# Storing the weight combinations of gate, up and Q in the first token half and loading them in the second

## Chip, cores, metric

One core of one Trainium2 chip. The metric is the device time of one execution in microseconds (us). The time before is 733.7 us, the median of three runs (732.07 to 734.33); with the runs made beside the changed kernel it is 732.96.

## The reference

```python
def reference(A_x, A_wqkv, A_wo, B_x, B_w_gate, B_w_up, B_w_down):   # S = 2048, D = 1024, F = 3584
    x = A_x
    xn = _layernorm(x)
    s = linear_attention(xn, A_wqkv, A_wo)      # 32 heads, phi(q), phi(k), kv and z sums over tokens; cut
    g = silu((silu(xn @ B_w_gate) * (xn @ B_w_up)) @ B_w_down)
    return x + s * g                            # bf16
```

## The kernel before

The kernel does its matrix products by a seven-product (Strassen-like) scheme. Each product of a 2x2 block matrix needs *combinations* of weight blocks (sums and differences), made by VectorE (DVE), and combinations of the results, read from PSUM. For the products "1" and "5" of gate, up and Q the scheme is applied a second time (the code calls it `joint`), so these need *inner* combinations too.

The tokens are worked off in two halves `p = 0, 1`. Order of the work: K and V and their state (0 to about 134 us), then for each half Q/gate/up in pairs of column tiles and after it the down-projection. Every weight tile of gate, up and Q is loaded twice, and its combinations are made twice. This is the part that the change touches:

```python
def sums(A, o, rd, wr):                      # four DVE subtractions or additions
    tt(rd, [wr[0]], o[0], A[0, 1], A[1, 1], ALU.add, True)
    tt(rd + [wr[0]], [wr[1]], o[1], o[0], A[0, 0], ALU.subtract, True)
    tt(rd, [wr[2]], o[2], A[0, 0], A[0, 1], ALU.subtract, True)
    tt(rd + [wr[1]], [wr[3]], o[3], A[1, 0], o[1], ALU.subtract, True)

def wload(src, joint):
    s = raw_ring.take()                      # 8 KB a partition, the raw tile, 1 MB
    dma([], [s.r], ..., src, dsem("wr%d" % s.k), 1024 * KB)
    c = cmb_ring.take()                      # 8 KB a partition: the outer combinations
    sums({...}, [cv[:, q] for q in range(4)], [s.r], cr)          # 4 x 128x1024
    # ... cut
    for m in joint:                          # (1, 5), or () for the very first Q tile
        t = in_ring.take()                   # 2 KB a partition: inner combinations
        sums(A, [tv[:, q] for q in range(4)], [r], tr)            # 4 x 128x256
```

The kernel does not issue its instructions in the order of this code. It collects all of them and runs a *list scheduler* in the build: a small model of five engines and one DMA queue decides the order of the instructions on each engine. Each engine then works strictly through that order on the chip, waiting on semaphores. The model has a rate for DMA, and a lead time for loads. (The byte count of a transfer enters a second time, in the deadline by which it is to be issued: 4.0 us + bytes / 200e3 before its first use. That line was not changed.)

```python
for o in ops:                                # every DMA: not before this PE instruction
    if o.sem is not None and o.succs:
        k = bisect_right(cum, o.dl - self.lead) - 1
        if k >= 0 and pes[k] not in o.preds:
            o.preds.add(pes[k])
# ... cut; in the loop that places one instruction after the other:
            if o.sem is not None:
                free[e] = s + 0.08
                b = max(s + 1.0, dma_free)
                dma_free = b + o.nbytes / 230e3      # MODELLED bytes per us of the one queue
                o.done = dma_free + 1.8
```

In the third pair of tiles (`n == 2`) of each half, the kernel also normalises Q: it reads reciprocals back from DRAM with a partition broadcast (`H<-r_scratch`, 16 transfers of 128 KB a half) and writes Q to `q_scratch` (2 MB a half).

## Time and profile before

| | before |
|---|---|
| time, median | 733.7 us |
| PE (TensorE) busy | 717.3 of 731.5 us, 98% |
| DVE busy | 596.5 us, 82% |
| ACT (ScalarE) busy | 397.7 us, 54% |
| DMA traffic | 94.0 MB |

The page of the kernel before: busy times and, in 40 slices, the tenths of PE and DVE and the granted clock.

```profile
span 731.5 us, 10526 instructions
...
PE 717.3 (98%) x3894; PEld 365.9 (50%) x3894; DVE 596.5 (82%) x1395; ACT 397.7 (54%) x743; POOL 14.1 (2%) x35
...
PE   8999999999999999999999999999999999999996
...
DVE  6999868979989998787457889999899988757353
...
PEclk9999999999999999999999999999999999999999
```

PE is busy everywhere, DVE nearly so in the Q/gate/up stages. The windows view of two stretches of the second half's Q/gate/up (columns: busy time and number of instructions of PE, PEld, DVE, ACT and POOL, then the granted clock, the DMA share, GB/s):

```profile
440.00:460.00 20.00, 19.46 (x113) 10.73 (x112) 20.00 (x52) 13.14 (x27) 0.00 (x0) 1.00 0.44 134
540.00:600.00 60.00, 60.00 (x349) 33.97 (x348) 55.76 (x139) 36.61 (x76) 0.00 (x0) 1.00 0.42 136
```

In the first, DVE is busy for all 20 us and PE loses 0.5. In the second, DVE is busy for 93% and PE loses nothing.

### The profile page before, as it was taken

The page shows a single profiled execution, that of the slowest core. Times are in us where ns is not written, and L with a number is a line of the kernel's source. Part 1 is how long each engine was busy: PE and PEld are TensorE (multiplying, and loading weights), DVE is VectorE, ACT ScalarE, POOL GpSimd, SP SyncE. Part 2 cuts the span into 40 slices and gives each one's busy share as a digit, 9 for nine tenths or more (in the row PEclk, how much of TensorE's full clock was granted, in tenths as well). Part 3 has the DMA queues.
Part 4 walks back from the last instruction along what each step waited for, and adds up shares of the span by engine and source line. Part 5 has one row for each costly group of instructions (what it writes and reads, how often), then busy time and mean ns, then how long its engine had stood idle before and what let it go on. Part 6 is the DMA issues. An engine that isn't in the chain of part 4 may idle for free.

```text
span 731.5 us, 10526 instructions
## 1 busy us (share of the span) xinstructions
PE 717.3 (98%) x3894; PEld 365.9 (50%) x3894; DVE 596.5 (82%) x1395; ACT 397.7 (54%) x743; POOL 14.1 (2%) x35
## 2 busy tenths in 40 slices
PE   8999999999999999999999999999999999999996
PEld 3444445455555555544444455555455554444442
DVE  6999868979989998787457889999899988757353
ACT  3776654787659766623232376767786654223231
POOL 2111000000000000000000000000000000000000
PEclk9999999999999999999999999999999999999999
DMA  9443235135257432471846534132835245274822
GB/s 293 110 102 86 44 111 176 59 109 166 75 149 217 156 109 65 130 216 32 213 118 153 170 86 152 59 116 76 245 145 173 74 136 167 77 166 118 177 65 50
DMA packets 135219, 94.00 MB, mean 129 GB/s; under 512 B 32512, under 2 KB 131072, under 8 KB 135168
## 3 DMA queue, kind: packets, MB, share of 16 engines
q1 hardware_dynamic: 135168, 93.34, 44.9%
q8 instruction: 30, 0.49, 0.3%
q14 instruction: 21, 0.17, 0.1%
HBM read 75.50 MB, written 10.62 MB: 118 GB/s over the span
## 4 chain that ended last, share of the span: by engine, by line
PE 86%; DVE 6%; ACT 4%; DMA 2%; issue 1%; POOL 0%; SPq 0%; ACTq 0%; DVEq 0%
PE ps L210 86%; ACT TM L341 2%; ACT H L341 2%; DMA W<-in_B_w_up_dram 1%; DVE H L717 1%; DVE W L348 1%; DVE ps L348 1%; DVE stats L642 1%; DVE TM L348 1%; DVE H L348 1%; ACT L341 1%; DVE TM L716 0%; DVE stats L646 0%; DMA W<-in_A_x_dram 0%; ACT ps L341 0%
## 5 line engine op out<-in xcount | busy, mean ns | idle before, releaser
L210 PE MATMUL ps<-X,W 128*128 128x512 f16 (+1 forms) x1408 | 312.0, 361 | 0.9 <-DVE ps L348 0.5
L341 ACT ACTIVATE TM<-ps 128x512 f16<-128x512 f32 (+2 forms) x337 | 181.7, 556 | 152.6 <-PE ps L210 148.5
L210 PE MATMUL ps<-H,W 128*128 128x512 f16 (+1 forms) x896 | 206.8, 379 | 0.3 <-DVE ps L348 0.3
L210 PEld LDWEIGHTS ps<-X,W 128*128 128x128 f16 (+1 forms) x1408 | 136.6, 98 | 122.2 <-DVE ps L348 2.3
L348 DVE TENSOR_TENSOR W<-W 128x256 f16<-128x256 f16 (+6 forms) x424 | 169.1, 440 | 9.7 <-DMA W<-in_B_w_down_dram 5.7
L348 DVE TENSOR_TENSOR ps<-ps,TM 128x256 f32<-128x256 f32 (+1 forms) x218 | 117.1, 540 | 33.1 <-PE ps L210 32.2
L210 PEld LDWEIGHTS ps<-H,W 128*128 128x128 f16 (+1 forms) x896 | 87.2, 98 | 103.4 <-DVE ps L348 0.7
L341 ACT ACTIVATE ps<-ps 128x512 f32<-128x512 f32 (+1 forms) x156 | 78.6, 504 | 59.3 <-PE ps L210 55.6
L341 ACT ACTIVATE H<-ps 128x512 f16<-128x512 f32 (+1 forms) x126 | 74.9, 602 | 57.4 <-PE ps L210 57.2
L210 PE MATMUL ps<-P,W 128*128 128x256 f16 (+1 forms) x440 | 90.0, 323 | 0.1
L210 PE MATMUL ps<-W 128*128 128x256 f16 (+1 forms) x328 | 69.7, 299 | 2.2 <-DVE ps L348 1.7
L348 DVE TENSOR_TENSOR TM<-ps,TM 128x512 f32<-128x512 f32 (+1 forms) x60 | 40.8, 681 | 29.4 <-PE ps L210 28.8
L341 ACT ACTIVATE TM<-TM 128x512 f16<-128x512 f32 (+1 forms) x61 | 37.9, 621 | 44.1 <-DVE TM L348 43.6
L210 PEld LDWEIGHTS ps<-P,W 128*128 128x128 f16 (+1 forms) x440 | 42.9, 98 | 32.9 <-DVE H L717 0.5
L348 DVE TENSOR_TENSOR H<-H,TM 128x512 f16<-128x512 f16 x112 | 45.2, 417 | 12.7 <-ACT H L341 12.4
L348 DVE TENSOR_TENSOR H<-H 128x1024 f16<-128x1024 f16 (+2 forms) x82 | 50.5, 629 | 0.6 <-DMA H<-in_A_wqkv_dram 0.3
L210 PEld LDWEIGHTS ps<-W 128*128 128x128 f16 (+1 forms) x328 | 30.8, 98 | 27.9 <-DVE ps L348 3.5
L348 DVE TENSOR_TENSOR TM<-TM 128x512 f16<-128x512 f16 (+1 forms) x59 | 24.2, 419 | 18.3 <-DMA TM<-TM 10.7
L210 PE MATMUL ps<-H,X 128*128 128x512 bf16 (+1 forms) x136 | 32.2, 379 | 1.2 <-ACT X L341 0.8
L210 PE MATMUL ps<-TM,W 128*128 128x256 f16 (+1 forms) x144 | 30.9, 296 | 0.3 <-DVE ps L348 0.3
L348 DVE TENSOR_TENSOR W<-H 128x1024 f16<-128x1024 f16 x40 | 26.9, 685 | 3.0 <-PE ps L210 2.8
L716 DVE TENSOR_SCALAR TM<-TM 128x512 f16<-128x512 f16 x64 | 17.7, 285 | 10.3 <-ACT TM L341 10.1
(81 smaller groups left out, 413.1 us busy)
## 6 DMA issues: line engine op xcount, KB each, us to landing
W<-in_B_w_gate_dram SPq DMA_DIRECT2D x14, 1024.0 KB, 5.3
W<-in_B_w_up_dram SPq DMA_DIRECT2D x14, 1024.0 KB, 5.5
W<-in_B_w_down_dram SPq DMA_DIRECT2D x16, 896.0 KB, 6.1
W<-in_A_x_dram SPq DMA_DIRECT2D x16, 256.0 KB, 3.0
H<-in_A_wqkv_dram SPq DMA_DIRECT2D x8, 512.0 KB, 8.3
W<-in_A_wqkv_dram SPq DMA_DIRECT2D x4, 1024.0 KB, 5.2
H<-r_scratch SPq DMA_DIRECT2D x32, 128.0 KB, 4.0
q_scratch<-H SPq DMA_DIRECT2D x8, 512.0 KB, 4.0
```

The source lines that it names most:

```text
L210: last = h.matmul(o, l, r, start=st, stop=sp, skip_group_check=True)
L341: return PL.op("act", reads, writes, lambda h: h.activation(o, i, func, **kw), nel(o) / 1200.0 + (0.055 if src == "ps" else 0.095))
L348: return dve(reads, writes, lambda h: h.tensor_tensor(o, a, b, op), nel(o), 1.92 if fast else 0.96)
L642: o0 = dve([s.r], [sA], lambda h: h.bn_stats(stats[:, j, 0, :], xa[:, 0:512]), 512)
L716: dve([e.r], [b.r], lambda h: h.tensor_scalar(ba, ea, 1.0, EPS_PHI, ALU.min, ALU.add), 512, 2.6)
L717: dve([src_r, b.r], [out_r], lambda h: h.scalar_tensor_tensor(out_ap, src, 0.0, ba, ALU.max, ALU.add), 512)
```

## The change

Intent: make the combinations once, in the first half, store them in DRAM (1 MB a tile, and two times 256 KB of inner ones), and load them in the second half, so that DVE has less to do there. The two constants of the scheduler's model were raised with it. The swap of two PSUM allocations in `Joint.step` came along too. Core of the diff:

```diff
-                dma_free = b + o.nbytes / 230e3
+                dma_free = b + o.nbytes / 320e3
-def build_kernel(nc, ..., LEAD=12.0):
+def build_kernel(nc, ..., LEAD=16.0):
+        c_scr = nc.dram_tensor("c_scratch", [16, 128, 4096], FP16)
+        i_scr = nc.dram_tensor("i_scratch", [16, 2, 128, 1024], FP16)
@@ Joint.step @@
-                    self.x, self.y = balloc(), balloc(True)
-                    x, y = self.x, self.y
+                    y = self.y = balloc(True)
+                    x = self.x = balloc()
@@
+        kept = {}
+        def combine(p, key, t, scr, make):
+            if key in kept:
+                dma([named(*key)], [t.r], t.ap(FP16), scr, dsem("cl..."), t.size * 128)      # load
+                return
+            make()
+            if p == 0:
+                kept[key] = True
+                dma([t.r], [named(*key)], scr, t.ap(FP16), dsem("cs..."), t.size * 128)      # store
@@ wload @@
-            sums({...}, [cv[:, q] for q in range(4)], [s.r], cr)
+            combine(p, ("c", n), c, c_scr[n], lambda: sums({...}, ...))
-                sums(A, [tv[:, q] for q in range(4)], [r], tr)
+                combine(p, ("i", n, m), t, i_scr[n, ...], partial(sums, A, ...))
```

The diff also brings code for a third joint product, "6" (`put6`, `LINK6`, places for its inputs). The lists that would switch it on stay `((1, 5), (1, 5))`, so it never runs.

More of the change, by code (lines that the diff above doesn't have):

```diff
@@ L218, in _tr_group, with build_kernel @@
     return last
-def build_kernel(nc, A_x, A_wqkv, A_wo, B_w_gate, B_w_up, B_w_down, out, WINDOW=6, NWARM=14, NPE=4, LEAD=12.0):
+def build_kernel(nc, A_x, A_wqkv, A_wo, B_w_gate, B_w_up, B_w_down, out, WINDOW=6, NWARM=14, NPE=4, LEAD=16.0):
     S, D, FF = 2048, 1024, 3584
@@ L480, in grp @@
                     pe_mm(reads, [bank_r[b]], mms)
+            s1_ring = None
             def put1(self, a):
                 self.a = a
+                if self.s1_ring is not None:
+                    self.s1 = self.s1_ring.take()
+                    act([bank_r[a]], [self.s1.r], self.s1.ap(F32), ps[a][:, :], ACT.Identity)
+                    return
                 self.b = balloc()
@@ L490, in put5, with put6, add5 @@
                 bfree(e)
+            def put6(self, b):
+                self.b = b
+                tt([bank_r[b], self.s1.r], [bank_r[b]], ps[b][:, :], ps[b][:, :], self.s1.ap(F32), ALU.add)
+                self.add5()
+            def add5(self):
+                self.c = balloc()
+                tt([bank_r[self.b], self.s5.r], [bank_r[self.c]], ps[self.c][:, :], ps[self.b][:, :],
+                   self.s5.ap(F32), ALU.add)
             def step(self, m):
@@ L505, in step @@
                     self.grp(6, self.b, False)
-                    self.c = balloc()
-                    tt([bank_r[self.b], self.s5.r], [bank_r[self.c]], ps[self.c][:, :], ps[self.b][:, :],
-                       self.s5.ap(F32), ALU.add)
+                    self.add5()
                 elif m == 7:
@@ L524, in build_kernel @@
         QJ = (((), (1, 5)), ((1, 5), (1, 5)))
+        GJ = ((1, 5), (1, 5))
         class Joint:
@@ L582, in build_kernel @@
         LINK = "7_0 nj1a 3_0 7_1 nj1b nj5a 3_1 nj1c nj5b 4_0 nj1d nj5c 4_1 n2_0 nj5d n6_0 n2_1 n6_1".split()
+        LINK6 = ("nj1a 7_0 3_0 nj1b nj5a 7_1 nj1c 3_1 nj5b nj1d nj6a 4_0 nj5c nj6b 4_1 nj5d nj6c n2_0 nj6d n2_1").split()
         last_pair = [None]
@@ L595, in feed @@
             else:
-                for w in LINK:
+                for w in LINK6 if "6" in pair.joint else LINK:
                     if w[0] == "n":
@@ L933, in build_kernel, with wload @@
         SUM_OF = {5: 0, 6: 1, 7: 2, 3: 3}
-        def wload(src, joint):
+        kept = {}
+        def combine(p, key, t, scr, make):
+            if key in kept:
+                dma([named(*key)], [t.r], t.ap(FP16), scr, dsem("cl%s%d" % (t.a.name, t.off // KB)), t.size * 128)
+                return
+            make()
+            if p == 0:
+                kept[key] = True
+                dma([t.r], [named(*key)], scr, t.ap(FP16), dsem("cs%s%d" % (t.a.name, t.off // KB)), t.size * 128)
+        def wload(p, n, src, joint):
             s = raw_ring.take()
@@ L943, in wload @@
             cr = [c.sub(q * 2 * KB, 2 * KB).r for q in range(4)]
-            sums({(k, i): v[:, :, 4 * k:4 * k + 4, i * 128:i * 128 + 128] for k in range(2) for i in range(2)},
-                 [cv[:, q] for q in range(4)], [s.r], cr)
+            combine(p, ("c", n), c, c_scr[n], lambda: sums(
+                {(k, i): v[:, :, 4 * k:4 * k + 4, i * 128:i * 128 + 128] for k in range(2) for i in range(2)},
+                [cv[:, q] for q in range(4)], [s.r], cr))
             def block(m):
@@ L962, in wload @@
                 A = {(k, i): bl[:, i, 2 * k:2 * k + 2, :] for k in range(2) for i in range(2)}
-                sums(A, [tv[:, q] for q in range(4)], [r], tr)
+                combine(p, ("i", n, m), t, i_scr[n, (1, 5).index(m)] if m < 6 else None,
+                        partial(sums, A, [tv[:, q] for q in range(4)], [r], tr))
                 inner[m] = (A, r, tv, tr)
@@ L978, in xset, with x_inner, joint_of @@
             return Set(ops, evac, dring)
-        IN_AT = (((W, 48 * KB), (W, 49 * KB), (W, 50 * KB)), ((W, 51 * KB), (TM, 8 * KB), (TM, 9 * KB)))
+        IN_AT = {1: (None, (W, 48 * KB), (W, 49 * KB), (W, 50 * KB)), 5: (None, (W, 51 * KB), (TM, 8 * KB), (TM, 9 * KB)),
+                 6: ((X, 10 * KB), (X, 11 * KB), (X, 12 * KB), (X, 13 * KB))}
+        s1_places = Places([(X, 14 * KB), (TM, 24 * KB)], 2 * KB)
         xin = {}
-        def x_inner(v):
-            for m, at in zip((1, 5), IN_AT):
+        def x_inner(v, ms):
+            for m in ms:
                 ap, r = v[XOF[m]]
                 B = {(k, j): ap[:, 2 * k:2 * k + 2, 256 * j:256 * j + 256] for k in range(2) for j in range(2)}
-                t = [(a.at(o, KB, FP16).rearrange("p (k t) -> p k t", t=256), a.reg(o, KB)) for a, o in at]
-                tt([r], [t[1][1]], t[1][0], B[1, 1], B[0, 1], ALU.subtract, True)
-                tt([r], [r], B[0, 1], B[0, 1], B[0, 0], ALU.subtract, True)
-                tt([r], [t[0][1]], t[0][0], B[1, 1], B[0, 1], ALU.subtract, True)
-                tt([r, t[0][1]], [t[2][1]], t[2][0], B[1, 0], t[0][0], ALU.subtract, True)
-                xin[m] = {1: (B[0, 0], r), 2: (B[1, 0], r), 3: (B[1, 1], r), 5: (B[0, 1], r), 6: t[0], 7: t[1], 4: t[2]}
-        def joint_of(jstat, s0, s1):
+                t1, t2, t3, t4 = ((B[0, 1], r) if at is None else
+                                  (at[0].at(at[1], KB, FP16).rearrange("p (k t) -> p k t", t=256), at[0].reg(at[1], KB))
+                                  for at in IN_AT[m])
+                tt([r], [t3[1]], t3[0], B[1, 1], B[0, 1], ALU.subtract, True)
+                tt([r], [t1[1]], t1[0], B[0, 1], B[0, 0], ALU.subtract, True)
+                tt([r, t1[1]], [t2[1]], t2[0], B[1, 1], t1[0], ALU.subtract, True)
+                tt([r, t2[1]], [t4[1]], t4[0], B[1, 0], t2[0], ALU.subtract, True)
+                xin[m] = {1: (B[0, 0], r), 2: (B[1, 0], r), 3: (B[1, 1], r), 5: t1, 6: t2, 7: t3, 4: t4}
+        def joint_of(jstat, s0, s1, ms):
             def ops(m):
@@ L1001, in ops @@
                 return f
-            return {"1": Joint(ops(1), lambda w, b: (s0, s1)[w].put1(b)),
-                    "5": Joint(ops(5), lambda w, b: (s0, s1)[w].put5(b))}
+            if 6 in ms:
+                s0.s1_ring = s1.s1_ring = s1_places
+            return {str(m): Joint(ops(m), lambda w, b, m=m: getattr((s0, s1)[w], "put%d" % m)(b)) for m in ms}
         later = deque()
@@ L1021, in q_load @@
         def q_load(p, s):
-            return wload(wqkv_v[:, :, s * 512:(s + 1) * 512], QJ[p][s])
+            return wload(p, 14 + s, wqkv_v[:, :, s * 512:(s + 1) * 512], QJ[p][s])
         PQ0 = 52 * KB
@@ L1039, in q_pair @@
             s0, s1 = (xset(stat, w, XV[p], evac(w), d_ring) for w in range(2))
-            pair = Pair(s0, s1, joint_of(jstat, s0, s1) if QJ[p][s] else None, at)
+            pair = Pair(s0, s1, joint_of(jstat, s0, s1, QJ[p][s]) if QJ[p][s] else None, at)
             if go:
@@ L1107, in hb2, with gu_load @@
             return v, Region(hb(n, nm)[1].keys + hb(n + 1, nm)[1].keys)
-        def gu_load(k, n):
-            return wload((wg_v if k == "g" else wu_v)[:, :, n * 512:(n + 1) * 512], (1, 5))
+        def gu_load(p, k, n):
+            return wload(p, 7 * (k == "u") + n, (wg_v if k == "g" else wu_v)[:, :, n * 512:(n + 1) * 512], GJ[p])
         sgs = {}
@@ L1143, in gu_pair @@
                 s0.direct, s1.direct = direct(0), direct(1)
-            feed(Pair(s0, s1, joint_of(jstat, s0, s1), at))
+            feed(Pair(s0, s1, joint_of(jstat, s0, s1, GJ[p]), at))
         def h_sums(n):
@@ L1328, in pump @@
                 k, p, s = lq.popleft()
-                got[k, p, s] = q_load(p, s) if k == "q" else gu_load(k, s)
+                got[k, p, s] = q_load(p, s) if k == "q" else gu_load(p, k, s)
         pump(2)
@@ L1343, in turn_pass @@
             combos(XV[1])
-            x_inner(XV[1])
+            x_inner(XV[1], (1, 5))
             gate[0] = 1
@@ L1372, in build_kernel @@
                 if (p, k, n) == (0, "q", 0):
-                    x_inner(XV[0])
+                    x_inner(XV[0], (1, 5))
                 pump(1)
```

## The prediction

> **What bounds the kernel now.** TensorE's instruction stream. The page's busy table gives PE 717 of 731.5 us (98%), DVE 596 (82%), ACT 398 (54%); the clock row is 9 throughout. A busy PE need not be at its peak, so I looked at matmul starts in the timeline: back to back, a 512-column matmul starts every 216 ns, a 256-column one every 108. The Trainium skill ("TensorE: Matmul & The Clock Gate", Part 1) states N/2.4 GHz plus about 2.5 ns for a warm array, 215.7 ns at 512; this trace agrees. Summing start-to-start time above those spacings gives PE's real slack: about 5 us in the first 32 us, 2.6 near 133-139 us (start of the first half's Q/gate/up), about zero in both down-projection stages (306-420, 610-722), 5.0 in the second half's Q/gate/up (422-610), 2.3 at the end. In 422-610 the pieces are 1.5 us at 521 and 0.1-0.7 each at 422, 432, 435, 443, 469, 479, 531-534.
>
> **What the change does.** The joint products stay (1, 5) for every pair and the joint-6 code is never reached, so every matmul stays. In the second half it removes the DVE sums of 16 weight tiles: four 128x1024 at 681 ns and, for gate/up and one Q tile, eight 128x256 at 281 ns: 4.97 us of a pair's 11.7, about 77 us in all. DVE should fall from 596 to about 520 us, and its share in 540-600 us from 93% to 50-55%. It adds about 23.5 MB of stores in the first half and as much of loads in the second: DMA traffic from 94 to about 143 MB. It also starts loads up to 4 us earlier (LEAD) and swaps two PSUM allocations.
>
> **How much is on the critical path.** Almost none. The 77 us can buy at most the 5 us above (0.7%). I expect 2 to 3: the waits at 431-443 and 469-479, where DVE is full (the windows view shows 20.0 of 20 us in 440-460), should go. The wait at 521 differs: a 1 MB up-weight load took 9.9 us to land instead of 5.5, because the broadcasts from r_scratch were in the queues, and DVE, then PE, waited.
>
> **What it may cost.** A second-half pair now needs 2.5 MB in place of 1 MB per 11.7 us, 224 GB/s. The DMA share and GB/s columns put full queues at about 300-330 GB/s for weight loads (my estimate from 0.82 at 251 and 0.32 at 105), so the steady state fits at about 70%. At n=2 the broadcasts (2 MB, about 200 GB/s while all engines are busy) and q_scratch stores (2 MB) come on top: an estimated 33 us of DMA work in two pairs, 23 us. The inner-combination buffers free only about one pair before use. I expect stalls of 1 to 4 us around 510-535 us in place of today's 1.5, and up to 2 us in the first half, where stores share one queue with loads and SP waits in order for DVE.
>
> **Prediction.** Gains and stalls nearly cancel: 732.5 us, 8 in 10 between 727.5 and 739. Faster by over 2%: 0.01; within 2%: 0.94; slower by over 2%: 0.05.
>
> **What would show it.** Right: matmul count equal, PE busy within 1% of 717, DVE near 520, DMA near 143 MB, the small PE waits before 480 us gone, the down-projection stages equally long. The balance is decided around 510-535 us: PE waiting there for scratch or weight loads. Wrong if PE waits for loads in the steady state (540-600 us), the queue order or true DMA rate being worse than I think (slower); or if matmul spacing falls when DVE is lighter (faster), of which the down-projection stages, DVE light and spacing 216 ns too, show nothing.

## The result

| | before | after |
|---|---|---|
| median of 4 runs | 732.96 us | 737.61 us |
| ratio | | 1.0063, 95% interval 1.0043 to 1.0083 |
| span of the profiled run | 731.5 | 736.5 |
| DVE busy | 596.5 | 543.7 |
| DMA traffic | 94.0 MB | 143.3 MB |

A ratio is the mean time of one kernel's fast runs over that of the other's of the same rounds, so it is not quite the ratio of the medians. The changed kernel is 4.65 us slower. The page after:

```profile
span 736.5 us, 10437 instructions
...
PE 716.4 (97%) x3880; PEld 366.6 (50%) x3894; DVE 543.7 (74%) x1211; ACT 396.6 (54%) x743; POOL 14.3 (2%) x35
...
PE   7999999899999999999999989999999999999996
...
DVE  6999867979989998796447775856875568746443
...
PEclk9999999999999999999999999999999999999999
```

The number of weight loads (PEld) is 3894 in both, so TensorE's work is the same. (14 matmul records are missing from the second trace.) 184 DVE instructions went, as expected. The same two windows after:

```profile
440.00:460.00 20.00, 20.00 (x118) 11.39 (x117) 11.46 (x25) 14.65 (x30) 0.00 (x0) 1.00 0.79 265
540.00:600.00 60.00, 60.00 (x350) 34.06 (x349) 37.26 (x75) 38.39 (x81) 0.00 (x0) 1.00 0.77 270
```

DVE fell from 93% to 62% in the steady state, the DMA share rose from 0.42 to 0.77, and PE lost nothing in either case. So neither the gain nor the loss is there.

**Where the time went.** Both traces hold all 3894 weight loads in their order, and the total work up to the end of a stage is the same. So the start of the k-th weight load in one trace less that in the other is the lag at that point. (Within a stage the order differs, and lags of a few tenths mean nothing.) I worked these lags out of the timeline:

| point (k-th weight load) | before, at us | after lags by |
|---|---|---|
| end of the K/V stage (720) | 133.9 | 0.2 us |
| first half, before the broadcasts (1200) | 215.8 | 0.2 |
| first half, after them (1440) | 256.9 | 2.3 |
| second block of its down-projection (2040) | 373.8 | 2.3 |
| near its end (2280) | 423.8 | 3.9 |
| second half, after the turn (2400) | 446.8 | 4.8 |
| second half, before its broadcasts (2760) | 505.0 | 4.3 |
| after them (3000) | 547.7 | 2.8 |
| second down-projection (3480) | 636.0 | 2.8 |
| last weight load (3893) | 727.1 | 4.0 |

After the last weight load 1.0 us more is lost in the order of the last outputs (4.4 us to the end before, 5.4 after). In the second half 1.9 us came back between 2400 and 3000 (before rounding). (That this is the freed DVE would be too quick: e1 below, with all sums still made, regains 1.9 us there, most of it because the up-weight load is no longer late.) They were more than eaten by losses in places where the change has no combinations to load: the first half's broadcasts (2.1), the two down-projections (1.6 and 1.2), and the end (1.0). At the turn into the second half another 0.9 went.

The loss of 1.6 us in the first down-projection shows its mechanism. First, before, around 385 us: DMA issues on SP, then DVE. (A line of the timeline has the start, the duration, the engine, the line of the code, the operation, output<-input, and in brackets how long the engine stood idle before it and who ended that.)

```profile
378.35 0.37 SPq L351 DMA_DIRECT2D W<-in_B_w_down_dram  x1
378.77 2.43 SPq L1250 DMA_TRANSPOSE TM<-TM  x1
381.24 0.58 SPq L351 DMA_DIRECT2D W<-m_scratch  x1
381.86 0.89 SPq L351 DMA_DIRECT2D W<-in_B_w_down_dram  x1
```

```profile
385.26 0.70 DVE L348 TENSOR_TENSOR ps<-ps,TM 128x512 f32<-128x512 f32 x1 [5.56 <-PE ps L210]
385.87 0.41 DVE L348 TENSOR_TENSOR TM<-TM 128x512 bf16<-128x512 f16 x1
387.40 0.43 DVE L348 TENSOR_TENSOR TM<-TM 128x512 f16<-128x512 f16 x1 [1.12 <-ACT TM L341]
387.75 1.55 DVE L348 TENSOR_TENSOR W<-W 128x512 f16<-128x512 f16 x4
391.31 0.69 DVE L348 TENSOR_TENSOR TM<-ps,TM 128x512 f32<-128x512 f32 x1 [2.01 <-PE ps L210]
391.92 1.69 DVE L348 TENSOR_TENSOR W<-W 128x896 f16<-128x896 bf16 x3
```

DVE first serves PSUM (`ps<-ps`), makes the combinations of the small matrix (`128x512`), and comes to those of w_down (`128x896`) last, at 391.9, without waiting for either load. After:

```profile
378.55 1.56 SPq L353 DMA_DIRECT2D W<-in_B_w_down_dram  x2
380.90 4.55 SPq L1289 DMA_TRANSPOSE TM<-TM  x1
385.49 0.60 SPq L353 DMA_DIRECT2D W<-m_scratch  x1
```

```profile
388.23 0.62 DVE L350 TENSOR_TENSOR W<-W 128x896 f16<-128x896 bf16 x1 [6.90 <-DMA W<-in_B_w_down_dram]
388.78 0.42 DVE L350 TENSOR_TENSOR TM<-TM 128x512 bf16<-128x512 f16 x1
389.11 0.62 DVE L350 TENSOR_TENSOR W<-W 128x896 f16<-128x896 bf16 x1
389.65 0.69 DVE L350 TENSOR_TENSOR ps<-ps,TM 128x512 f32<-128x512 f32 x1
...
390.40 0.82 PE L210 MATMUL ps<-H,W 128*128 128x512 f16 x3 [1.39 <-DVE ps L350]
```

The scheduler has put the w_down combinations ahead of the PSUM addition. DVE waits 6.9 us in order for a load that landed late, the PSUM addition stands behind it, and PE waits 1.39 us for that addition. The second w_down load landed at 388.2, 9.0 us after its issue. In the kernel before it landed later still, at 389.9 (8.0 us after its issue), and delayed nobody, because DVE came to it only at 391.9. Over the whole trace, DVE's waits for w_down went from 5.7 us in 3 places to 21.9 in 5.

The other clear change of order is at the first half's broadcasts. SP before, then after:

```profile
211.39 0.40 SPq L351 DMA_DIRECT2D W<-in_B_w_up_dram  x1
214.20 5.62 SPq L351 DMA_DIRECT2D H<-r_scratch  x8
```

```profile
210.50 1.74 SPq L353 DMA_DIRECT2D H<-r_scratch  x4
212.29 0.43 SPq L353 DMA_DIRECT2D W<-in_B_w_up_dram  x1
214.39 2.17 SPq L353 DMA_DIRECT2D H<-r_scratch  x4
```

Four broadcasts now go ahead of the up-weight load. In after, DVE waited 1.6 us for that load between 205 and 240 us, and PE 1.5 us for DVE; before, neither waited there.

### The profile page after: what moved, and what is told of

The parts are those of the page before. It is cut to its first block, busy times and chain, and to the rows that moved or that the text cites. A ratio compares the mean times of both kernels' runs of the same rounds, so it can differ in the third digit from the quotient of the medians.

```text
span 736.5 us, 10437 instructions
## 1 busy us (share of the span) xinstructions
PE 716.4 (97%) x3880; PEld 366.6 (50%) x3894; DVE 543.7 (74%) x1211; ACT 396.6 (54%) x743; POOL 14.3 (2%) x35
## 4 chain that ended last, share of the span: by engine, by line
PE 82%; DMA 7%; DVE 4%; ACT 4%; issue 1%; SPq 1%; ACTq 0%; DVEq 0%
PE ps L210 82%; DMA W<-in_B_w_down_dram 3%; ACT H L343 1%; ACT TM L343 1%; DMA W<-i_scratch 1%; DMA H<-in_A_wqkv_dram 1%; DVE ps L350 1%; DMA W<-m_scratch 1%; DMA H<-r_scratch 1%; DVE W L350 1%; SPq L353 1%; DVE H L350 1%; DVE H L736 1%; DMA W<-in_A_x_dram 1%; DVE TM L350 1%
## 5 line engine op out<-in xcount | busy, mean ns | idle before, releaser
L350 DVE TENSOR_TENSOR W<-W 128x256 f16<-128x256 f16 (+6 forms) x284 | 121.4, 463 | 28.1 <-DMA W<-in_B_w_down_dram 21.9
L210 PEld LDWEIGHTS ps<-P,W 128*128 128x128 bf16 (+1 forms) x440 | 42.8, 98 | 34.8 <-DVE TM L350 2.0
L350 DVE TENSOR_TENSOR H<-ps,TM 128x512 f16<-128x512 f32 (+1 forms) x35 | 24.0, 685 | 3.3 <-PE ps L210 2.3
```

The costliest lines, as they stand in the source:

```text
L210: last = h.matmul(o, l, r, start=st, stop=sp, skip_group_check=True)
L350: return dve(reads, writes, lambda h: h.tensor_tensor(o, a, b, op), nel(o), 1.92 if fast else 0.96)
```

## Experiments

Twelve kernels were run; all but e4 and e12 gave correct results. "Before" in each measurement is the kernel before, run in the same rounds. My first theory (A) was: the stores cost the first half its 2 us, the scheduler's constants cost the down-projections their 3. Rivals: all of the loss is DMA traffic (B), or all of it is the constants (C). The code of the constants can be changed without the scratch and the other way round, so the two were crossed.

### e1: only the constants

```diff
 (kernel before)
-                dma_free = b + o.nbytes / 230e3
+                dma_free = b + o.nbytes / 320e3
-LEAD=12.0
+LEAD=16.0
```

> The kernel before with only the scheduler's two constants of the change (LEAD 16, DMA model 320). Theory A (traffic and constants share the loss: stores cost 2 us at 222-236 us of the first half, constants about 2.8 us in the down-projection stages at 388, 660 and 700 us and 1 at the end): 2 to 4 us slower than before, with the same stalls of PE waiting for w_down combinations in the down-projection stages. Rival B (all the loss is DMA traffic): 733, no change, no stall in the down-projection stages. Rival C (constants alone explain everything): 737 to 738.

Measured: 737.28 us, ratio 1.0063 (1.0050 to 1.0076). That is the whole loss of the change, without a byte of scratch. B falls, and A was too small on this side. The profile (of a run at 735.9, the fastest of the six) has the stall in the down-projection that after has. DVE's waits in 366 to 400 us of e1:

```profile
DVE W L348 <- DMA W<-in_B_w_down_dram: 7.2, 1, 7.2
```

It also loses 3.0 us at the first half's broadcasts (k = 1200 to 1440), so the stores of the scratch are not what after lost there.

### e2: the scratch with the constants of before

```diff
 (kernel after)
-                dma_free = b + o.nbytes / 320e3
+                dma_free = b + o.nbytes / 230e3
-LEAD=16.0
+LEAD=12.0
```

> The kernel after with the scheduler's constants of before (LEAD 12, DMA model 230). Theory A: the down-projection stalls go, the stall at 222-236 us and the gain after 440 us stay: 733 to 735 us. Rival B: stays at 737 to 738. Rival C: 730 to 732, as the freed DVE then pays its 2 to 3 us.

Measured: 746.67 us, ratio 1.0201 (1.0186 to 1.0215). No theory of mine had this; C falls too as a sum of independent parts. The lag is 9 us by the end of the first half's Q/gate/up (k = 1680), where PE waited 4.0 us for DVE's PSUM additions and 3.6 for DVE's weight sums. The scratch adds 1.5 MB of stores to 1 MB of load in each pair of 11.7 us, about 224 GB/s (2.5 x 1.048 MB over 11.7 us). A model that gives the queue 230 GB/s has no room left for that and the broadcasts. That the model then delays loads in its plan is my inference from these two numbers; the plan itself was not measured. Shown is only that 230/12 and the scratch don't go together, and that with the scratch the new constants take 9.1 us off.

### e3: stores, but no loads

```diff
 (kernel after, combine)
-            if key in kept:
+            if False:
```

> The kernel after, but the second half recomputes all sums as before did: stores stay, loads go, DVE is not freed. Theory A: the first half's loss of about 2 us stays, the second half loses its gain of 2 us and its loss of 1 us at the turn: 737 to 740 us. If loads in the second half were what costs: 734 to 736.

Measured: 740.05 us, ratio 1.0104 (1.0087 to 1.0122), just over the expected 737 to 740. Against e1 (same constants, no scratch) the stores cost 2.8 us; against after, the loads and the freed DVE give back 2.4. Its trace lags 4.3 us at k = 3000 where after lags 2.8; it is that of the fastest of the six runs (737.96) and loses only 1.1 us at the first half's broadcasts.

### e4: freed DVE alone

In the second half the sums of the 14 gate and up tiles are left out, and stale combinations are used. Its output is wrong, which doesn't matter for the time. No scratch, constants of before.

```diff
 (kernel before, wload)
+            if ("c", n) not in kept or n > 13:          # kept: made in the first half; Q is still computed
                 sums({...})
```

> Wrong result on purpose: the kernel before, with the sums of the 14 gate and up tiles of the second half simply left out (stale combinations are used), no stores, no loads, constants of before. This is what freed DVE time alone is worth. Theory A (PE bound, 5 us of slack in that stage): 729 to 732 us, DVE about 526 us. Rival D (DVE load slows PE in a way that start-to-start times don't show): below 725 us.

Measured: 731.27 us, ratio 0.9983 (0.9971 to 0.9995). The trace lies within 0.02 us of the kernel before until the turn, and ends 2.2 us ahead. DVE was busy for 548.6 us. So 48 us of freed DVE time, with no traffic at all, are worth 1.4 us by the clock. That is what the intent could buy in the order of before, with TensorE's work unchanged and no traffic; other orders were not tried this way. Rival D falls. The windows of e4:

```profile
440.00:460.00 20.00, 20.00 (x119) 11.51 (x118) 14.84 (x35) 12.98 (x27) 0.00 (x0) 1.00 0.38 120
540.00:600.00 60.00, 60.00 (x350) 34.09 (x349) 36.43 (x72) 36.84 (x78) 0.00 (x0) 1.00 0.39 123
```

### e5 and e6: one constant at a time

New theory (E): the rate makes the scheduler place DVE and ACT work behind loads that have not landed; LEAD lets the broadcasts out ahead of the up-weight load, which cannot go earlier because its buffer is not free. e5 is e1 with LEAD at 12, e6 is e1 with the rate at 230.

> The kernel before, only the scheduler's DMA rate raised from 230 to 320. Theory E (the higher rate makes the scheduler place in-order DVE and ACT work behind loads that have not landed; this causes the stall of 1.7 us at about 388 us, where DVE waits 7 us for w_down): the 388 stall is here, the 216-236 loss is not: 734.5 to 736 us. If rate is harmless: 732 to 733.5.

> The kernel before, only LEAD raised from 12 to 16. Theory E (LEAD lets the r_scratch broadcasts out 3 to 4 us earlier, ahead of the up-weight load, whose buffer is not free earlier; DVE then waits for that load): the loss of 2 to 3.4 us at 216-236 us is here, the 388 stall is not: 735 to 737 us. If LEAD is harmless: 732 to 733.5.

Measured: e5 737.69 us, ratio 1.0066 (1.0046 to 1.0085); e6 734.03, ratio 1.0024 (1.0009 to 1.0039). The rate alone costs as much as both constants; LEAD alone costs little. But the way differs. The granted clocks of the runs, 0.993 to 0.996 in all six of e5, stand for 4.0 us lost to a lower clock on average (one less the clock, times the span), against 0.9 in the kernel before of the same rounds. In e1 it is 1.8 against 1.1. Some of this is a drop after the last matmul, where it costs nothing (in the profiles 1.6 us in e5, 1.4 in e1, 1.0 in before). So 2 to 3 of e5's 4.7 us are a lower clock, and most of e1's loss is not. And the stages were not those that E named. e5 has no stall at 388 us (its lag stays at 3.1 us from k = 2040 to 2280); it lost 2.6 us in the K/V stage, of which 1.7 are 3.4 us at half the clock (see e8), and at the second half's broadcasts (k = 2760 to 3000) it lost 0.6 us where e1 regained 1.3. DVE's waits for w_down did grow to 16.9 us in e5 and not in e6 (2.6 us). e6 keeps the broadcasts ahead of the up-weight load in its order, and yet DVE waits only 0.3 us for that load there (1.6 in after). So E is right that the rate is what hurts, and wrong about where each constant acts.

### e7: after, with the broadcasts as late as before

```diff
 (kernel after, Plan.schedule)
-                k = bisect_right(cum, o.dl - self.lead) - 1
+                k = bisect_right(cum, o.dl - self.lead + o.late) - 1     # late = 4.0 for r_scratch, else 0
```

> The kernel after, but the r_scratch stores and broadcasts keep their old lead of 12 us, so that in the first half the up-weight load is again issued ahead of the broadcasts. Theory E: the loss at 222-236 us goes (about 2 us), the rest stays: 735 to 736.5 us. If the stores of the new scratch cause that loss: stays at 737 to 738.

Measured: 738.42 us, ratio 1.0077 (1.0059 to 1.0095): no gain. In its trace the loss at the first half's broadcasts did fall, from 2.1 us to 0.5 (k = 1200 to 1440). But 1.5 us appeared at the start of that half, where the clock dropped in this profile (1.7 us, see e8), and the second half's broadcasts lost 0.5 us where after regained 1.5. The order does cause the stall, and mending one order by hand moved others.

### e8: after, with slow transfers counted as slow

The rate of 320 stays, LEAD stays at 16, and five kinds of transfer are counted with more bytes than they move. That these are slower can be seen on the page of before, for instance in the last column here (us from issue to landing): a w_down load takes longer than a gate load that is larger.

```profile
W<-in_B_w_gate_dram SPq DMA_DIRECT2D x14, 1024.0 KB, 5.3
W<-in_B_w_down_dram SPq DMA_DIRECT2D x16, 896.0 KB, 6.1
```

```diff
 (kernel after; the byte counts that only the scheduler reads)
-  w_down load          896 * KB
+  w_down load         1147 * KB
-  r_scratch broadcast  128 * KB
+  r_scratch broadcast  205 * KB
-  m_scratch load       512 * KB
+  m_scratch load       655 * KB
-  residual in, out     256 * KB
+  residual in, out     328 * KB
```

> The kernel after, but the scheduler counts the slow transfers (broadcasts, w_down, m_scratch, the 512-byte-row input and output) at 200 to 250 in place of 320. Theory E: DVE is no longer placed behind w_down loads that have not landed, the stalls at 388, 660 and 700 us go (2.8 us): 733 to 735.5 us. Rival F (any reordering by the list scheduler moves a few us by luck): no stage changes in the way named, some other stall appears.

Measured: 733.50 us, ratio 1.0018 (1.0000 to 1.0037). Five of the six runs lie between 732.67 and 734.47; the sixth, the profiled one, took 737.66. DVE's waits for w_down fell from 21.9 us to 4.2. In the trace the lag is flat through both down-projections (2.4 from k = 2040 to 2280, 3.8 from 3000 to the end), so the losses of 1.6 and 1.2 us are gone, as expected. At the first half's broadcasts 1.6 us are still lost. About 4 of the change's 4.65 us are therefore the scheduler's belief that every transfer runs at 320 GB/s. One thing was overlooked: the added bytes also move the deadlines (by the code's bytes / 200e3, a w_down load is to be issued 1.3 us earlier). Whether the later believed landing or the earlier issue does the work was not separated.

The profile suggests why its own run was slow. PE waited 2.25 us for a scratch load at the turn, and after that wait the clock was halved for a while:

```profile
430.00:440.00 10.00, 7.22 (x36) 3.14 (x35) 6.75 (x16) 6.74 (x12) 0.00 (x0) 0.98 0.72 196
440.00:450.00 10.00, 10.00 (x51) 5.41 (x50) 6.41 (x13) 6.41 (x11) 0.00 (x0) 0.85 0.79 252
...
438.03 0.38 PE L210 MATMUL ps<-P,W 128*128 128x256 f16 x2 [2.25 <-DMA W<-c_scratch]
...
441.86 1.63 PE L210 MATMUL ps<-X,W 128*128 128x512 f16 x4
```

In the trace's clock records the drop is 3.4 us at half the clock, so 1.7 us less work. One of the same length appears in the profiled runs of e5 (0.83 in 10 to 20 us), e7 and e9 (0.86 in 140 to 150) as well, right after gaps of PE (1.73 us in e5, 1.18 and 0.86 in e7 and e9). In after there is none before the last outputs, though it has the same two gaps of 1.18 and 0.86. It can explain part of the spread of the kernels with stalls: after such a gap the loss may grow by 1.7 us.

### e9: e8 with the turn mended

The first gate tile's combinations are neither stored nor loaded, because their buffer comes free only when the last down-projection block ends.

```diff
 (e8, combine)
-            if p == 0:
+            if p == 0 and key[1] != 0:
```

> The kernel of e8_real_rates, but the first gate tile's combinations are neither stored nor loaded: DVE makes them again at the turn, where the profiles of after and of e8 show TensorE waiting 1.5 to 2.3 us at 435-437 us for that tile's scratch load, whose buffer comes free only when the last down-projection block ends. If that load is the cause: the wait goes, 731 to 732.5 us, about level with the kernel before or slightly under it. If the turn is bound by something else (ACT or DVE evacuations): no change from e8, 733 to 734.

Measured: 733.52 us, ratio 1.0012 (0.9997 to 1.0027). The wait for the scratch load is gone from the trace: the longest wait of PE in 425 to 445 us is 0.6. The median did not move. In the profiled run only this one and one of 0.2 us stand in that stretch, and the lag does not grow there (2.9 at k = 2280 and at 2400). Its 1.7 us of halved clock at 139 to 143 us lie elsewhere. That the turn's load is worth 1.5 us is not confirmed.

### e10: a placebo

The kernel before with the rate at 240 in place of 230, to see what any change of order costs (rival F).

> The kernel before with the scheduler's DMA rate at 240 in place of 230, a change with no meaning of its own. Rival F (the list scheduler's order is sensitive, any change of the constants costs luckily or unluckily up to a few us against the tuned pair 230 and 12): 734 to 737 us. If the order depends smoothly on the constants: 732.5 to 733.5.

Measured: 733.06 us, ratio 1.0007 (0.9994 to 1.0020): no change. The order is not so brittle that any touch costs 4 us. A rate of 320 does. But stages do move: the placebo's trace lags by 1.6 us from the first half on, and gets them back at the second half's broadcasts, where the up-weight load lands in 7.1 us instead of 9.9. So 1 or 2 us in a single stage say little.

### e11: e8 without the scratch

> The kernel before (no scratch) with the scheduler's constants and slow-transfer counts of e8_real_rates. Against e8 it gives the net worth of stores, loads and freed DVE under one cost model. If freed DVE pays and traffic is hidden: 735 to 736, 2 us slower than e8. If traffic costs more than DVE gives: 731 to 733.

Measured: 732.46 us, ratio 1.0004 (0.9989 to 1.0019). With e1 this is the cleanest pair of all: the same kernel, the same 320 and 16; the only difference is how the scheduler counts the slow transfers (in their landing and their deadline). 737.28 becomes 732.46. DVE's waits for w_down, e1 first, then e11, over the whole trace:

```profile
DVE W L348 <- DMA W<-in_B_w_down_dram: 21.6, 7, 7.2
```

```profile
DVE W L348 <- DMA W<-in_B_w_down_dram: 8.1, 6, 2.8
```

Against e8 it gives what scratch and freed DVE are worth under one model of the transfers: 732.46 without, 733.50 with. The intervals of the two ratios overlap (0.9989 to 1.0019 and 1.0000 to 1.0037), so the scratch costs between nothing and a few tenths of a per cent. No gain is shown.

### e12: spending the freed DVE time on the third joint product

```diff
 (e9)
-        GJ = ((1, 5), (1, 5))
+        GJ = ((1, 5), (1, 5, 6))
-            x_inner(XV[1], (1, 5))
+            x_inner(XV[1], (1, 5, 6))
```

> The kernel of e9_turn_fix with the joint product 6 switched on for gate and up in the second half, which spends the freed DVE time on less TensorE work: per pair 8 matmuls of 512 columns give way to 14 of 256, 216 ns less by the measured spacings, 3.0 us in 14 pairs. If TensorE's stream is what bounds the stage: 3 us less than e9, 728 to 730 us. If the extra DVE work or PSUM traffic fills what was freed: no gain, 731 to 735.

Measured: 741.24 us, ratio 1.0118, and a wrong result (relative error 12), which was not intended. The inputs of product 6 go to the places that the changed kernel has for them (`IN_AT`), which by the code overlap residual buffers of the first half's last down-projection block; I filled them at the turn, before those buffers are written. That this is the error is read from the code and not tested. Its profile shows PE waiting for DVE's additions (3.0 us in all) and for several kinds of ACT evacuation (2.0 to 2.6 us each). Whether the product pays when it is placed rightly stays open.

### The runs together

| scheduler's model | without scratch | with scratch |
|---|---|---|
| 230, LEAD 12 | 732.96 (before) | 746.67 (e2) |
| 320, LEAD 16 | 737.28 (e1) | 737.61 (after) |
| 320, LEAD 16, slow transfers counted as slow | 732.46 (e11) | 733.50 (e8) |

No correct version beat the kernel before clear of noise.

## Why the prediction was right and where it was not

The time, 737.61 us, fell into the range of 727.5 to 739 and into "within 2%". It lies 5.1 us above the 732.5 named and 1.4 under the upper edge: the loss comes from a term that the prediction did not count, and that it was no larger than the range allowed is luck. Point by point:

- **TensorE's stream bounds the kernel, and freed DVE time can buy almost nothing: right.** e4 is the direct measurement: 1.4 us, for 48 us less of DVE. In the second half of after, the lag falls by 1.9 us between k = 2400 and 3000, about the "2 to 3" that I expected, but e1 regains 1.9 us there with DVE as full as before. So the gain that I gave to DVE is not shown to be DVE's in after; e4 alone shows its worth.
- **DVE near 520 us: off, 543.7.** All 184 instructions went, but 77 us of them was a sum of mean durations, and neighbouring DVE instructions overlap: two 128x1024 ones in a row took 1.29 us in the timeline, not 1.36, and start 0.61 us apart. By start-to-start times (0.61 and, for 128x256, 0.20 us) the estimate would have been 64 x 0.61 + 120 x 0.20 = 63 us; measured were 53, and the last 10 are not explained. In 540 to 600 us its share fell to 62%, not to 50 to 55. The Trainium skill ("Perfetto Trace Analysis", Optimizing Scalar/DVE Operations) says just this: a profiled duration holds about twice the per-instruction overhead of about 60 ns, because its second half overlaps the next instruction. This trace roughly agrees, with 70 to 80 ns of overlap an instruction (0.681 less 0.61, 0.281 less 0.20). I should have costed with starts, as I did for TensorE.
- **Traffic of 143 MB, and a steady state that holds: right.** PE lost nothing in 540 to 600 us at a DMA share of 0.77.
- **"I expect stalls of 1 to 4 us around 510-535 us in place of today's 1.5": wrong in sign.** The 1.5 us wait for the up-weight load went, and the lag fell by 1.5 us there.
- **"Up to 2 us in the first half, where stores share one queue with loads": right in size (2.1), wrong in cause.** e1 loses 3.0 us in the same place with no stores. (Stores do cost: 2.8 us by e3 against e1, but its trace does not put them there.)
- **"The down-projection stages equally long": wrong, and this is the step that failed.** They lost 1.6 and 1.2 us, and the end 1.0. I listed LEAD as a gain ("starts loads up to 4 us earlier") and gave the DMA rate of the scheduler no cost at all. The mis-sized term of the sum is that one: counted as 0, it is +4.6 us (e1 against before of the same rounds, 737.28 less 732.69), and 4.7 by e5 with the rate alone (737.69 less 732.99). The rest of my sum, gain against stalls, came out as I had it, near zero: after less e1 is 0.3 us, and e8 less e11 is 1.0. That holds for these two models; under 230/12 the scratch costs 14 us (e2).

What stays open: which stall belongs to which constant, and why the rate alone (e5) lost about half of its time as a lower clock. E's assignment was wrong for both, and the same few us turned up in different stages in e1, e5 and e7. What is settled is that the belief of 320 GB/s for all transfers costs 4 to 5 us with or without the scratch, and that counting the slow ones as slow takes it away in both.

## What to carry to other kernels

Before taking work off an engine, measure how long the bounding engine waits for it; an engine at 93% that nobody waits for has nothing to give. Where a scheduler in the build fixes the order, its constants are part of the kernel: a rate that is too high for some transfers can put in-order engines in front of loads that have not landed (DVE's 6.9 us at 388 us), in stages that the change does not touch. Cross the change with its constants (four kernels) before believing what either did.

## What the Trainium skill lacked or had wrong

- "DMA: Bandwidth & Descriptors", Specifications, gives 512 bytes as the smallest transfer for line rate. In the trace of after, the median time of a packet grows as 18 ns for 256 bytes, 27 for 512, 46 for 1024, 84 for 2048, 309 for 8192. Over 16 engines (16 x bytes / time) that is 228, 303, 356, 390 and 424 GB/s: 512-byte packets run at about 70% of 8 KB ones. (The skill does say elsewhere that small transfers carry an overhead; "Perfetto Trace Analysis", DMA Optimizations, does so for those under 2 KB, without a size.) Under a full load of w_down reads and transposes with some output writes (351 to 359 us of before) the queue moved 253 GB/s at a share of 1.09, and of weight and scratch loads (541 to 559 us of after) 359 at 0.98.
- "TensorE: Matmul & The Clock Gate", Part 1, has the clock fall to half after at least one idle window of about 3.4 us. In e8 a drop followed a wait of 2.25 us (with 0.34 and 0.19 us near it), and in e7 two gaps of 1.18 and 0.86 us within 3 us: the granted clock was 0.52 in 140 to 143 us of e7. The trace of after has the same two gaps (137.8 and 139.2 us) and no drop. So gaps well under that window can do it in some runs. Part 1 does say further on that frequent short idles can throttle the clock; what it lacks is how short.
